# Interleaving the first two query passes of an attention kernel in halves of the keys, with the second half projected later

## The chip, the cores and the metric

One core of one Trainium2 chip. The kernel before takes 510.46 us (510.23 to 510.75). "Span" is what the profile shows of one execution on the core; it is shorter than the device time of the same execution by 1.7 us in nearly all of them (510.06 us and 508.4 us for the profiled execution of the kernel before).

Engines: TensorE (PE, with its weight loads PEld), VectorE (DVE), ScalarE (ACT), GpSimd (POOL), SyncE (SP, which issues the transfers).

## The reference

Two attention blocks over 2048 tokens, 448 wide, 16 heads of 28, put side by side. Cut to what matters here:

```python
def _A_ref(x, wqkv, wo):                       # part A: full softmax attention
    q, k, v = ...                              # x @ wqkv, split in 16 heads
    scores = einsum('bhqd,bhkd->bhqk', q, k) * Dh ** -0.5
    p = softmax(scores)
    return einsum('bhqk,bhkd->bhqd', p, v)... @ wo
# part B: 4 segments of 512 tokens, each with masked softmax attention inside
# the segment and a linear-attention memory of the segments before it
return concatenate([a, b], axis=-1)
```

## The kernel before

The kernel schedules itself. A model of the engines in Python runs while the program is built, and emits instructions in the order in which the model finds them ready; every engine then runs its list in order. The chip's times don't feed back.

Scores are handled in "banks" of 128 keys by 512 queries of one head, 1184 in all: 1024 for part A (16 passes, each 4 heads by 512 queries by 16 key tiles) and 160 for part B. Most banks go to ScalarE, which takes the exponential of three and two banks in turn (`NBS`). Some, called vbanks, go to VectorE, which computes the exponential from integer and polynomial steps over pairs of banks. Three slots of PSUM, the memory that holds TensorE's results, serve everything else: accumulators of a pass, projections, and vbanks.

```python
NBS = (3, 2)
YB = 3          # buffers of a pair of vbanks; shared with the tiles of x (xn)
AHEAD = 12      # a side piece may run this many banks ahead of its place
SEM = 45        # model: ns for a semaphore
SLACK = 300
HEADQ = 2
LASTV = 18      # no vbank from a pass with fewer free banks than this
...
    order = []                                  # order of the score banks
    for n, (kind, a, b) in enumerate(SEQ):      # SEQ: (A,0,0), (A,0,1), (A,0,2), ...
        T[kind, a, b] = len(order)
        if kind == "A":
            order += [("A", a, b, kt, j) for kt in range(NT) for j in range(4)]
        ...
    def fuse(bs):                               # may the last score group be joined by vbanks?
        used = {b[4] for b in bs}
        if sum(x["pos"] < 0 for x in side_work) > HEADQ:   # head pieces still open
            return
        for _ in range(2):
            if backlog(m["top"]) > BACKLOG: return         # VectorE has enough to do
            s = free_slot(m["top"])
            if s is None: return                           # no PSUM slot
            b = vbank_pick(used)                           # buffers; LASTV; 24 of a pass at most
            if b is None: return
            emit_vbank(b, s)
...
    # what the first pass needs: transposes of x (t_piece), keys, values, queries
    head = [kq_piece("k", "A", 0, 0, P, 2 * P), kq_piece("k", "A", 0, 0, 2 * P, CW),
            t_piece(1, 0), t_piece(1, 1), k_("A", 0, 1),
            v_piece("A", (0, 1), 0), v_piece("A", (2, 3), 0),
            t_piece(2, 0), t_piece(2, 1), k_("A", 0, 2),
            v_piece("A", (4, 5), 0), v_piece("A", (6, 7), 0),
            t_piece(3, 0), t_piece(3, 1), k_("A", 0, 3)]
    head += [v_piece("A", (t, t + 1), 0) for t in range(8, 16, 2)] + [q_("A", 0, 1)]
    spread(head, -100, -50)                     # places before the first bank: at once
```

After the last scores, `last_step` and `last_finish` accumulate the last pass (tile `acc`, copied to `osb`), normalise it and multiply by the output weights (`y_mm`).

The softmax here doesn't subtract the row's maximum and nothing guards it: scores larger than these inputs give would overflow.

## Time and profile before

| | kernel before |
|---|---|
| time, median | 510.46 us |
| span of the profiled execution | 508.4 us |
| ScalarE busy | 492.9 us (97%) |
| TensorE / VectorE busy | 475.4 (94%) / 445.7 us (88%) |
| first exp starts | 8.32 us |
| exps on ScalarE | 211 of three banks, 210 of two, 1 of one = 1054 banks |
| vbanks on VectorE | 130 |

First the windows view of the kernel before: a row for each stretch of time, with its length, then the busy time and (in brackets) the instructions of each engine, the granted clock of TensorE (the share of its full clock that the profile reports), the DMA share and GB/s.

```profile
8.00:40.00 32.00, 31.69 (x380) 14.78 (x377) 15.08 (x25) 31.25 (x28) 8.42 (x17) 1.00 0.28 68
40.00:300.00 260.00, 243.42 (x2573) 83.23 (x2572) 246.97 (x410) 260.00 (x234) 67.94 (x79) 1.00 0.13 32
300.00:490.00 190.00, 180.18 (x1783) 61.79 (x1786) 170.62 (x318) 189.00 (x172) 60.03 (x91) 1.00 0.20 56
```

The order of the engines is PE, PEld, DVE, ACT, POOL. ScalarE (fourth) is busy 260.00 of 260.00 us in the long middle. VectorE (third) is idle for half of the first stretch, in which TensorE is full.

Then ScalarE's groups of instructions by shape: count, busy time of the group, mean length of one, and the idle time before them.

```profile
L561 ACT ACTIVATE pt<-ps_s 128x1536 bf16<-128x1536 f32 x211 | 326.6, 1548 | 1.8 <-PE ps_s L280 1.3 <-PE ps_v_5806 L280 0.4
L561 ACT ACTIVATE pt<-ps_s 128x1024 bf16<-128x1024 f32 x210 | 237.1, 1129 | 0.1
...
L561 ACT ACTIVATE pt<-ps_s 128x512 bf16<-128x512 f32 x1 | 0.7, 672 | 0.0
```

The three groups sum to 564.4 us, while all exps together kept ScalarE busy for 480.4 us: in the trace one exp overlaps the next, by an estimated 0.2 us (84 us over 421 changes from one to the next). So the lengths can't simply be added.

And ScalarE's timeline, cut to the rows in which it was idle before an exp or before the last accumulation: start, length of the run of instructions, and in brackets the idle time before it with what ended it.

```profile
8.32 6.88 ACT L561 ACTIVATE pt<-ps_s 128x1536 bf16<-128x1536 f32 x6 [0.53 <-PE ps_s L280]
15.54 53.63 ACT L561 ACTIVATE pt<-ps_s 128x1536 bf16<-128x1536 f32 x47 [0.33 <-PE ps_s L280]
...
336.12 6.88 ACT L561 ACTIVATE pt<-ps_s 128x1536 bf16<-128x1536 f32 x6 [0.40 <-PE ps_v_5806 L280]
...
412.33 85.61 ACT L561 ACTIVATE pt<-ps_s 128x1536 bf16<-128x1536 f32 x76 [0.47 <-PE ps_s L280]
500.43 0.78 ACT L1195 COPY osb<-acc 128x128 f32<-128x128 f32 x4 [2.48 <-PE acc L280]
```

This gives an account of the whole span. It has four terms:

- **start**: until the first exp, 8.32 us;
- **stalls** of ScalarE between first and last exp: 0.33 + 0.40 + 0.47 = 1.20 us;
- **tail**: from the end of the last exp (500.43 - 2.48 = 497.95 us) to the end of the span, 10.45 us;
- **net work**: the rest, 488.43 us, in which ScalarE runs its exps and a few other activations without a pause that this view shows.

### The profile page before, as it was taken

The numbers are of one execution on the slowest core, as the hardware profiler recorded it, in microseconds if no ns is written. First come the engines' busy times: TensorE is split into PE (matmuls) and PEld (weight loads), VectorE is DVE, ScalarE is ACT, GpSimd is POOL, SyncE is SP. The second block draws the span as 40 slices with busy tenths as digits, with TensorE's granted clock in tenths as the row PEclk, the third lists the DMA queues.
The fourth block names the chain that finished last, engine by engine and source line by source line (L and its number), as shares of the span: only waits on it lengthen the run. The fifth ranks groups of instructions, "written<-read, shape, count | busy, mean of one in ns | idle before, by whom it ended". The sixth has DMA issues, their size and how long they took to land.

```text
span 508.4 us, 12361 instructions
## 1 busy us (share of the span) xinstructions
PE 475.4 (94%) x4918; PEld 168.6 (33%) x4918; DVE 445.7 (88%) x777; ACT 492.9 (97%) x450; POOL 144.6 (28%) x199
## 2 busy tenths in 40 slices
PE   8999999999999999999889999899999999999996
PEld 5443233343332333333223333433333333333332
DVE  4349999999999999989989989879979958998993
ACT  5999999999999999999999999999999999999993
POOL 8202211221122110351260431372161183202110
PEclk9999999999999999999999999999999999999999
DMA  9200000000033100022021102012312120312112
GB/s 249 56 1 5 22 13 13 3 22 4 23 109 73 37 9 3 23 66 48 20 66 46 44 6 65 23 31 65 101 52 57 50 76 18 108 50 60 39 48 65
DMA packets 42178, 23.76 MB, mean 47 GB/s; under 512 B 22636, under 2 KB 37804, under 8 KB 42120
## 3 DMA queue, kind: packets, MB, share of 16 engines
q1 hardware_dynamic: 40808, 21.72, 16.1%
q0 software_dynamic: 416, 0.81, 0.7%
q8 instruction: 38, 0.62, 0.5%
q10 hardware_dynamic: 896, 0.45, 0.3%
q14 instruction: 20, 0.16, 0.1%
HBM read 16.58 MB, written 4.28 MB: 41 GB/s over the span
## 4 chain that ended last, share of the span: by engine, by line
ACT 52%; PE 22%; issue 19%; DVE 5%; POOL 1%; DMA 1%; DVEq 0%; ACTq 0%; POOLq 0%
ACT pt L561 50%; PE ps_s L280 6%; PE acc L280 5%; PE ps_proj L280 3%; PE ps_v L280 2%; PE ps_y L280 2%; ACT phiq L1042 1%; PE ps_kn L280 1%; PE ps_warm L219 1%; DVE vy L458 1%; DVE y L1080 1%; POOL pt L579 1%; DVE vz L505 1%; DVE oT L753 1%; PE ps_t L1022 0%
## 5 line engine op out<-in xcount | busy, mean ns | idle before, releaser
L561 ACT ACTIVATE pt<-ps_s 128x1536 bf16<-128x1536 f32 (+1 forms) x422 | 480.4, 1337 | 2.0 <-PE ps_s L280 1.3
L280 PE MATMUL ps_s<-qTA,kTA 28*128 28x512 bf16 x894 | 141.1, 383 | 20.3 <-ACT pt L561 17.4
L513 POOL TENSOR_SCALAR vz<-vy 128x1024 f16<-128x1024 uint16 x59 | 71.0, 1203 | 290.6 <-DVE vy L458 147.0
L280 PE MATMUL acc<-pt,vA 128*32 128x512 bf16 x894 | 116.8, 386 | 0.0
L280 PEld LDWEIGHTS <-kTA 28*128 28x128 bf16 x1024 | 46.4, 91 | 144.1 <-issue 140.0
L495 DVE SCALAR_TENSOR_TENSOR ve<-vy,vz 128x1024 uint16<-128x1024 int32 x65 | 80.8, 1243 | 0.1
L579 POOL TENSOR_SCALAR_AFFINE_SELECT pt<-pt 128x256 bf16<-128x256 bf16 (+3 forms) x112 | 59.5, 559 | 54.4 <-ACT pt L561 54.3
L280 PE MATMUL acc<-warm 128*32 128x512 bf16 (+1 forms) x634 | 68.5, 384 | 0.0
L506 DVE TENSOR_TENSOR vz<-vz,vl 128x1024 f16<-128x1024 f16 x65 | 50.1, 770 | 0.1
L280 PEld LDWEIGHTS <-vA 128*32 128x32 bf16 x1024 | 31.7, 94 | 47.8 <-issue 41.1
L505 DVE TENSOR_TENSOR vz<-vz 128x1024 f16<-128x1024 f16 x65 | 47.2, 726 | 0.2
L280 PE MATMUL ps_proj<-xT_100,wst 128*32 128x512 bf16 x512 | 38.3, 383 | 0.1
L280 PE MATMUL ps_proj<-xT_99,wst 128*32 128x512 bf16 (+2 forms) x512 | 37.1, 374 | 0.3 <-DVE vy L458 0.2
L280 PE MATMUL acc<-ve,vA 128*32 128x512 bf16 x130 | 33.5, 383 | 0.0
L280 PEld LDWEIGHTS <-wst 128*32 128x32 bf16 x1024 | 22.4, 95 | 28.2 <-issue 18.4
L280 PE MATMUL ps_s<-qTB,kTB 28*128 28x384 bf16 (+3 forms) x256 | 25.7, 299 | 5.0 <-ACT pt L561 4.2
L509 DVE TENSOR_SCALAR vl<-vz 128x1024 f16<-128x1024 f16 x65 | 27.3, 420 | 1.2 <-POOL vz L513 1.2
L720 DVE COPY osb<-acc 128x512 f32<-128x512 f32 x31 | 21.2, 683 | 7.0 <-PE acc L280 7.0
L280 PEld LDWEIGHTS <-warm 128*32 128x32 bf16 (+1 forms) x642 | 18.9, 94 | 21.5 <-issue 15.3
L753 DVE TENSOR_TENSOR oT<-osb,bc 128x512 bf16<-128x512 f32 x31 | 24.7, 797 | 0.0
L280 PE MATMUL acc<-pt,vB 128*32 128x128 bf16 (+3 forms) x256 | 20.5, 303 | 0.6 <-POOL pt L579 0.4
L280 PE MATMUL ps_y<-woB,oT 128*128 128x448 bf16 x80 | 20.7, 356 | 0.2
(388 smaller groups left out, 496.9 us busy)
## 6 DMA issues: line engine op xcount, KB each, us to landing
out_dram<-y SPq DMA_DIRECT2D x31, 112.0 KB
xn<-in_A_x_dram SPq DMA_DIRECT2D x3, 448.0 KB
wst<-in_A_wqkv_dram SPq DMA_DIRECT2D x2, 249.0 KB
woA<-in_A_wo_dram POOLq DMA_DIRECT2D x4, 98.0 KB, 7.2
woB<-in_B_wo_dram POOLq DMA_DIRECT2D x4, 98.0 KB, 4.5
wst<-in_A_wqkv_dram SPq DMA_DIRECT2D x1, 336.0 KB
wst<-in_B_wv_dram SPq DMA_DIRECT2D x1, 336.0 KB
wst<-in_B_wk_dram SPq DMA_DIRECT2D x1, 336.0 KB
```

Of the source, the lines that this page charges most:

```text
L219: nc.tensor.matmul(wps[:], lhsT=warm[:, 0:P], rhs=warm[:], start=True, stop=True)
L280: nc.tensor.matmul(out, **kw)
L458: dve(e0, 0, 533, lambda: nc.vector.tensor_scalar(out=pr["y"][:, i, :], in0=ps[:], scalar1=Y1, scalar2=Y0, op0=ALU.mult, op1=ALU.add), aft ...
L495: step(t, 533 * n, lambda: nc.vector.scalar_tensor_tensor(out=ef.bitcast(U16), in0=y, scalar=2.0 ** -9, in1=z, op0=ALU.mult, op1=ALU.add), ...
L505: step(t, 267 * n, lambda: nc.vector.tensor_mul(z, z, z), lambda t: step(t, 267 * n, lambda: nc.vector.tensor_mul(z, z, l), whole))
L506: lambda t: step(t, 267 * n, lambda: nc.vector.tensor_mul(z, z, l), whole))
L509: step(t, 133 * n, lambda: nc.vector.tensor_scalar(out=l, in0=z, scalar1=Z3, scalar2=Z2, op0=ALU.mult, op1=ALU.add), square)
L513: eng.tensor_scalar(out=z, in0=y.bitcast(U16).rearrange("p (c t) -> p c t", t=2)[:, :, 0], scalar1=2.0 ** -16, scalar2=Z0, op0=ALU.mult, o ...
L561: nc.scalar.activation(out=pt[:, 0:n, :], in_=ps[:, 0:n, :], func=ACT.Exp, scale=scale)
L579: nc.gpsimd.affine_select(out=blk, in_=blk, compare_op=ALU.is_ge, fill=0.0, base=0, pattern=pat, channel_multiplier=-1)
L720: nc.vector.tensor_copy(out=os_[0][:], in_=a[:])
L753: nc.vector.tensor_mul(get_oT(side, s)[:, g, :], os_[0][:], bc[:])
```

## The change

The first two query passes of part A use the same keys and values. The change runs them interleaved: pass 0 with the first eight key tiles, pass 1 with the first eight, then pass 0 and pass 1 with the last eight. So keys and values of the second half are needed 32 banks later, and their transposes and projections leave the crowded head. TensorE gets room there, and VectorE may start on vbanks earlier. Since x tiles and vbank pairs share buffers, the count of used buffers (`ys`) starts at 3 and falls as each x tile has been transposed.

```diff
+SPLIT = 8
...
+    first = order[:128]
+    half = [[b for b in first if b[2] == cq and (b[3] < SPLIT) == lo] for cq in range(2)
+            for lo in (True, False)]
+    order[:128] = half[0] + half[2] + half[1] + half[3]
...
-    st = {"u": 0, "pos": 0, "ys": 0, "es": 0, "work": 0.0, "nrm": 0, "ot": 0}
+    st = {"u": 0, "pos": 0, "ys": 3, "es": 0, "work": 0.0, "nrm": 0, "ot": 0}
...
                 rt["x", "A", r, half] = e
+                st["ys"] -= half
...
-            t_piece(1, 0), t_piece(1, 1), k_("A", 0, 1),
-            v_piece("A", (0, 1), 0), v_piece("A", (2, 3), 0),
-            t_piece(2, 0), t_piece(2, 1), k_("A", 0, 2),
-            v_piece("A", (4, 5), 0), v_piece("A", (6, 7), 0),
-            t_piece(3, 0), t_piece(3, 1), k_("A", 0, 3)]
-    head += [v_piece("A", (t, t + 1), 0) for t in range(8, 16, 2)] + [q_("A", 0, 1)]
+            t_piece(1, 0), t_piece(1, 1), v_piece("A", (0, 1), 0), k_("A", 0, 1),
+            v_piece("A", (2, 3), 0), q_("A", 0, 1), v_piece("A", (4, 5), 0), v_piece("A", (6, 7), 0)]
     spread(head, -100, -50)
+    head = [t_piece(2, 0), t_piece(2, 1), k_("A", 0, 2), t_piece(3, 0), t_piece(3, 1)]
+    head += [v_piece("A", (8, 9), 0), k_("A", 0, 3)]
+    head += [v_piece("A", (t, t + 1), 0) for t in range(10, 16, 2)]
+    spread(head, 8, 8 * SPLIT + 8)
```

## The prediction

> **What bounds the kernel now.** ScalarE. The page gives it 492.9 us busy of a 508.4 us span (97%), almost all of it one group: 422 exp activations, 480.4 us. The windows view says where it is not busy: before its first exp at 8.32 us; 0.43 us between 8.32 and 40 us; nothing between 40 and 300; 1.0 us between 300 and 498; and 8.2 of the last 10.45 us, where it waits for the last accumulation (2.5 us in the waits view) and the closing matmuls. So the time is the start, plus ScalarE's exp work, plus its few stalls, plus the tail. VectorE (88%) takes 130 of the 1280 score banks off ScalarE. It is idle in one place only: between 8.32 and 40 us it is busy 15.1 of 31.7 us, waiting (waits view) 7.6 us for value projections and about 6 us for key/query projections. TensorE is then the busy one (31.4 of 31.7 us). From 40 us on VectorE is 93% busy.
>
> **What the change does.** With the first two query passes interleaved in halves of the keys, transposes and projections of the second key half are needed 32 banks later. Comparing the two built programs by matmul order: in the first 64 banks, 248 side matmuls in place of 284; the VectorE exps begin in the first 64 (5 banks; none before), stand at 14 against 11 after 128 and at 30 against 28 after 256. The catch: the lead does not last. After 640 banks both stand at 74, and the totals are 131 against 130. ScalarE keeps 211 three-bank and 210 two-bank exps and loses only the single one-bank exp. Projections, the passes' closing work, masks (110 instructions, the same number of blocks) and DMA are equal in number; 27 filler matmuls are added, in TensorE's slack. The gain goes back because the later picks are limited by buffers, by VectorE's backlog and by a cap per pass, not by how many banks were done early.
>
> **Cost.** By shapes, a three-bank exp takes 1548 ns, a two-bank one 1129 ns: 419 ns a bank. The Trainium skill, "ScalarE: Activation LUTs", section "What ACT_TABLE_LOAD costs", says 0.833 ns per element (427 ns for 512); the trace agrees. The 422 exps take 480.4 us for 1150 banks, which leaves an estimated 0.4 to 0.5 us for the lost bank with its instruction. All of that is on the critical path. The 0.43 us of early stalls, one of 0.33 us at 15.5 us, may go as well, as TensorE has less to do there. The first exp comes after the same instructions, so the start stays. VectorE's 17 us of early idle time are worth little: they are used now, but VectorE gets them back as slack later, off the path.
>
> The tail changes form: ScalarE's last unit has three banks in place of one, and VectorE's last piece is a half pair. I allow 1 us either way. The schedule behind the head is reshuffled too; new small stalls of ScalarE, as before 0 to 2 us, I put at 0.3 us.
>
> **Predicted:** 510.55 - 0.5 - 0.4 + 0.3, about 509.9 us; range 508.5 to 511.5. Faster by over 2%: 0.01; within 2%: 0.97; slower by over 2%: 0.02.
>
> **Right or wrong in the profile.** Right: first exp at 8.3 us; 421 exps, about 479.9 us; VectorE busy well over 15 us between 8 and 40 us, and less busy later; ScalarE gaps between first and last exp within 0.5 to 2 us; tail after the last exp 9.5 to 11.5 us. Wrong: a gap of over 1 us in ScalarE between 8 and 50 us, ended by score matmuls that stood behind a projection or a value tile waiting for VectorE or its PSUM slot, since two accumulators are held at once there and leave one slot of three.

Two figures in it are wrong and are put right here. "1280 score banks" and "1150 banks" counted score matmuls; a bank of part B can take two. There are 1184 banks, of which ScalarE has 1054 before. So the exps cost 480.4 / 1054 = 0.456 us a bank, and the "640" in the text is a count of matmuls too. The conclusions drawn from them about the lost bank don't change.

## More of the kernel before

The metric is the device time of one execution in microseconds, as the median of several executions.

Output projections of earlier passes (tile `ps_y`) are side pieces.

## The result

| | before | changed |
|---|---|---|
| time, median | 510.46 us (510.23 to 510.75) | 508.82 us (508.60 to 509.42) |
| ratio | | 0.9969 (0.9952 to 0.9987) |
| span of the profiled execution | 508.4 us | 506.9 us |
| ScalarE's banks | 1054 | 1053 |

A ratio is the mean time of one kernel's runs over that of the other's of the same rounds, so it isn't quite the ratio of the medians. The time fell by 1.6 us, 0.3%: inside the range of the prediction, and further than its centre of 509.9 us.

The windows of the changed kernel, with the same columns:

```profile
8.00:40.00 32.00, 30.74 (x363) 14.19 (x364) 23.66 (x39) 30.93 (x28) 10.55 (x19) 1.00 0.29 68
40.00:300.00 260.00, 245.03 (x2614) 84.23 (x2616) 245.72 (x406) 259.96 (x235) 67.30 (x80) 1.00 0.13 32
300.00:490.00 190.00, 180.70 (x1786) 61.72 (x1793) 171.13 (x318) 189.81 (x173) 59.61 (x89) 1.00 0.20 56
```

VectorE is busy 23.66 us in the first stretch, 8.6 us more. That is the intent fulfilled. ScalarE's busy time in that stretch did not change to match, because it was full before as well.

Its groups and idle rows:

```profile
L566 ACT ACTIVATE pt<-ps_s 128x1536 bf16<-128x1536 f32 x211 | 327.3, 1551 | 1.3 <-PE ps_s L281 1.1
L566 ACT ACTIVATE pt<-ps_s 128x1024 bf16<-128x1024 f32 x210 | 237.7, 1132 | 0.0
```

```profile
8.86 6.89 ACT L566 ACTIVATE pt<-ps_s 128x1536 bf16<-128x1536 f32 x6 [0.53 <-PE ps_s L281]
16.29 54.41 ACT L566 ACTIVATE pt<-ps_s 128x1536 bf16<-128x1536 f32 x48 [0.54 <-PE ps_s L281]
...
498.88 0.77 ACT L1201 COPY osb<-acc 128x128 f32<-128x128 f32 x4 [1.43 <-PE acc L281]
```

The account in the four terms (us, profiled executions):

| | start | net work | stalls | tail | span |
|---|---|---|---|---|---|
| before | 8.32 | 488.43 | 1.20 | 10.45 | 508.4 |
| changed | 8.86 | 488.05 | 0.54 | 9.45 | 506.9 |
| difference | +0.54 | -0.38 | -0.66 | -1.00 | -1.5 |

So with one bank fewer ScalarE's net work is 0.38 us less (the busy time of its exps fell from 480.4 to 479.9 us), and the two larger terms lie 300 us and more behind the place of the change: two stalls in part B (at 336 and 412 us) are gone, and the tail is shorter. The head's own stall did not go. It grew from 0.33 to 0.54 us.

**The start is not the change's doing.** TensorE's list is the same in both kernels up to the first scores. In the groups that read the x tiles (count, then least, median and greatest length in ns, and first and last start), the kernel before shows:

```profile
L227 PE MATMUL ps_h_171<-ident,xn x4: 219/267/314, 4.7 to 5.4; 128*128 128x128 bf16 x4
...
L227 PE MATMUL ps_h_174<-ident,xn x4: 219/219/219, 5.2 to 5.7; 128*128 128x128 bf16 x4
```

and the changed kernel:

```profile
L228 PE MATMUL ps_h_171<-ident,xn x4: 314/314/314, 4.7 to 5.6; 128*128 128x128 bf16 x4
...
L228 PE MATMUL ps_h_174<-ident,xn x4: 314/314/314, 5.3 to 6.3; 128*128 128x128 bf16 x4
```

The same transposes take 219 ns in one execution and 314 ns in another, from the start or from some transpose on. The Trainium skill, "TensorE: Matmul & The Clock Gate", section "What's actually happening", says that the clock of a cold TensorE doubles after a busy window that runs freely, so that the moment varies by about 500 ns either way between executions. The profiles agree: over the 14 kernels profiled the first exp starts between 7.97 and 8.92 us, with no clear order by kernel (8.32 to 8.92 us with the old head, 7.97 to 8.86 us with the new one). The start follows the mean length of the 16 transposes: 219 ns goes with 7.97 to 8.06 us (three profiles), 314 ns with 8.77 to 8.92 us (four, two of each kernel). The kernel before also spread over 507.9 to 509.1 us of span in its own runs. So a difference in one pair of profiles carries about half a microsecond of this either way.

### The profile page after: what moved, and what is told of

Read it like the earlier page. It is cut to its first block, busy times and chain, and to the rows that moved or that the text cites. A ratio compares the mean times of both kernels' runs of the same rounds, so it can differ in the third digit from the quotient of the medians.

```text
span 506.9 us, 12393 instructions
## 1 busy us (share of the span) xinstructions
PE 475.3 (94%) x4936; PEld 168.8 (33%) x4945; DVE 450.0 (89%) x782; ACT 492.5 (97%) x449; POOL 144.4 (28%) x200
## 4 chain that ended last, share of the span: by engine, by line
ACT 55%; issue 20%; PE 19%; DVE 4%; POOL 1%; DVEq 0%; ACTq 0%
ACT pt L566 54%; PE ps_s L281 5%; PE acc L281 4%; PE ps_proj L281 4%; PE ps_y L281 2%; PE ps_v L281 1%; ACT phiq L1048 1%; DVE vy L463 1%; PE ps_warm L220 1%; POOL pt L584 1%; DVE ve L500 0%; DVE vB L832 0%; DVE phik L877 0%; DVE vz L510 0%; DVE vz L511 0%
## 5 line engine op out<-in xcount | busy, mean ns | idle before, releaser
L566 ACT ACTIVATE pt<-ps_s 128x1536 bf16<-128x1536 f32 (+1 forms) x421 | 479.9, 1342 | 1.3 <-PE ps_s L281 1.1
L518 POOL TENSOR_SCALAR vz<-vy 128x1024 f16<-128x1024 uint16 (+1 forms) x60 | 74.5, 1242 | 295.3 <-DVE vy L463 166.0
L500 DVE SCALAR_TENSOR_TENSOR ve<-vy,vz 128x1024 uint16<-128x1024 int32 x66 | 84.3, 1280 | 0.2
L584 POOL TENSOR_SCALAR_AFFINE_SELECT pt<-pt 128x256 bf16<-128x256 bf16 (+3 forms) x112 | 55.7, 525 | 47.7 <-ACT pt L566 47.0
L281 PE MATMUL acc<-warm 128*32 128x512 bf16 x628 | 68.1, 384 | 0.3
L510 DVE TENSOR_TENSOR vz<-vz 128x1024 f16<-128x1024 f16 x66 | 48.5, 737 | 0.3
L281 PE MATMUL acc<-ve,vA 128*32 128x512 bf16 x131 | 35.9, 383 | 0.0
L281 PE MATMUL ps_s<-qTB,kTB 28*128 28x128 bf16 (+3 forms) x256 | 25.4, 299 | 5.5 <-ACT pt L566 4.8
L1086 DVE CAST y<-ps_y 128x448 bf16<-128x448 f32 x28 | 17.3, 619 | 6.2 <-PE ps_y L281 5.8
L758 DVE TENSOR_TENSOR oT<-osb,bc 128x512 bf16<-128x512 f32 x31 | 21.6, 697 | 0.0
L281 PE MATMUL acc<-pt,vB 128*32 128x384 bf16 (+3 forms) x256 | 21.2, 303 | 0.4 <-POOL pt L584 0.2
```

The source lines that it names most:

```text
L281: nc.tensor.matmul(out, **kw)
L500: step(t, 533 * n, lambda: nc.vector.scalar_tensor_tensor(out=ef.bitcast(U16), in0=y, scalar=2.0 ** -9, in1=z, op0=ALU.mult, op1=ALU.add), ...
L510: step(t, 267 * n, lambda: nc.vector.tensor_mul(z, z, z), lambda t: step(t, 267 * n, lambda: nc.vector.tensor_mul(z, z, l), whole))
L518: eng.tensor_scalar(out=z, in0=y.bitcast(U16).rearrange("p (c t) -> p c t", t=2)[:, :, 0], scalar1=2.0 ** -16, scalar2=Z0, op0=ALU.mult, o ...
L566: nc.scalar.activation(out=pt[:, 0:n, :], in_=ps[:, 0:n, :], func=ACT.Exp, scale=scale)
L584: nc.gpsimd.affine_select(out=blk, in_=blk, compare_op=ALU.is_ge, fill=0.0, base=0, pattern=pat, channel_multiplier=-1)
```

## The experiments

All of them change the order that the builder makes, so each was checked by its built program first (banks on each engine, last units), and these counts are in the expectations. Each was timed in five rounds beside the kernel before on the same chip. All twelve gave correct results.

### 1. Is it the early vbanks? VectorE kept out of the first 64 banks

```diff
         used = {b[4] for b in bs}
+        if st["pos"] < 64:
+            return
```

> The changed kernel, but VectorE may take no score bank while fewer than 64 banks have been passed. Built, VectorE takes 127 banks in all (changed kernel 131, before 130), so ScalarE has 4 more than in the changed kernel. Theory (the early banks are what the change earns): 4 banks at about 0.45 us each come back, 510.3 to 511.0 us, the VectorE idle time between 8 and 40 us returns in part. Rival (the gain is relief of TensorE in the head, or a luckier tail, and the early VectorE banks do not matter): within 0.5 us of the changed kernel, 508.5 to 509.3 us.

Measured: 512.41 us (512.31 to 516.71), the kernel before 510.40; ratio 1.0060 (1.0034 to 1.0086). VectorE's busy time in the first stretch fell to 12.94 us:

```profile
8.00:40.00 32.00, 31.75 (x362) 15.25 (x359) 12.94 (x21) 31.40 (x28) 7.38 (x16) 1.00 0.28 69
```

The rival is out: in this schedule, without the early vbanks, the kernel is slower than the kernel before by 2 us. The theory's sign was right and its size too small. Against the changed kernel, net work rose by 2.05 us for 4 banks, about as expected (1.8 us), and that alone is more than the gain of 1.64 us. The tail rose by 1.57 us and the stalls by 0.28 us, which had not been foreseen; the reshuffles below show that these two also move when nothing of substance is changed.

### 2. The interleaved order alone, with the old head

```diff
-            t_piece(1, 0), t_piece(1, 1), v_piece("A", (0, 1), 0), k_("A", 0, 1),
... (the head of the kernel before in place of that of the changed kernel)
+    head += [v_piece("A", (t, t + 1), 0) for t in range(8, 16, 2)] + [q_("A", 0, 1)]
```

> The interleaved order of the changed kernel with the old list of head pieces (all transposes, keys and values of the first pass at the old place). Built, VectorE takes 130 banks as before. Theory (interleaving alone earns nothing, only the deferral of head work that it permits): 510.2 to 511.5 us, with a ScalarE stall at the first bank of the second pass, as its query projection stands last in the list. Rival (the interleaving itself helps, by spreading the work): 508.5 to 509.5 us.

Measured: 517.99 us (517.78 to 518.22); ratio 1.0153 (1.0140 to 1.0166). ScalarE's waits (who ended them, total, times, longest):

```profile
ACT pt L566 <- PE ps_v L281: 8.6, 1, 8.6
```

TensorE's timeline before that wait ended:

```profile
24.14 1.71 PE L281 MATMUL ps_v<-wst,xT 128*128 128x224 bf16 x16
25.78 0.39 PE L281 MATMUL acc<-pt,vA 128*32 128x512 bf16 x2
25.80 1.23 PE L281 MATMUL ps_proj<-xT,wst 128*32 128x512 bf16 x16
26.97 1.80 PE L281 MATMUL ps_v<-wst,xT 128*128 128x224 bf16 x16
28.69 1.05 PE L281 MATMUL ps_proj<-xT,wst 128*32 128x512 bf16 x16
29.67 0.39 PE L281 MATMUL ps_s<-qTA,kTA 28*128 28x512 bf16 x2
```

The scores of the second pass stand behind the whole old head, because their query projection is its last piece. The Trainium skill, "PSUM — Partial Sum Buffer", section "Engine vs sequencer instructions", says that matmuls start and complete in program order; here that costs one stall of 8.57 us. The rest of the account (net 487.90, tail 11.27 us) adds up to about that of the kernel before: without this stall the span would be 507.8 us by subtraction, against 508.4. The direction was expected, the size was not (510.2 to 511.5 us): a stall had been foreseen, but not how long. So the interleaved order with this list loses by the place of one piece. A list with that query projection moved forward and nothing deferred was not run, so it isn't shown that interleaving alone earns nothing.

### 3. Two more vbanks for the changed kernel

```diff
-LASTV = 18
+LASTV = 17
```

> The changed kernel with the limit for picks in the last pass lowered from 18 free banks to 17. Built, VectorE takes 133 banks (131), ScalarE ends with a one-bank unit as the kernel before does. Theory (time is ScalarE's banks at 0.45 us plus the tail after its last exp): work 0.9 us less; the tail of 9.5 us may grow back to 10.5 us as before: 507.6 to 509.0 us. Rival (the count does not matter, the half pair in the tail does): slower than the changed kernel by about 1 us, 509.5 to 510 us.

Measured: 508.39 us (507.71 to 510.02); ratio 0.9971 (0.9956 to 0.9985), so it can't be told from the changed kernel. Net work fell by 1.25 us to 486.80, and the tail rose by 0.93 us to 10.38. Both parts of the theory came as said, and they nearly cancel.

### 4. The changed kernel's totals with the old head

```diff
-LASTV = 18
+LASTV = 16          # in the kernel before
```

> The kernel before with the limit for picks in the last pass lowered from 18 to 16. Built, it has the totals and the last units of the changed kernel (131 banks, last exps of 3, 2 and 3 banks), with the old head. Theory: what counts is the number of banks and the tail, wherever they are taken: about 508.8 to 509.7 us, close to the changed kernel. Rival (the head itself is faster in the changed kernel, whatever the count): 510.0 us or more.

Measured: 513.75 us (513.58 to 513.88); ratio 1.0069 (1.0057 to 1.0081). With the same 131 vbanks and the same last units as the changed kernel it is 5 us slower than that. Net work is 488.28 us, as the count says, but the theory's number (508.8 to 509.7 us) was far off, and the time lies where the rival put it (510.0 us or more). The account doesn't bear the rival out either: the start is within 0.06 us of the changed kernel's, the stalls are 1.90 us, 1.36 more (one of 1.04 us at 257 us), and the tail is 13.10 us, 3.65 more. So the tail is not given by the last units. ScalarE's waits:

```profile
ACT osb L1195 <- PE acc L280: 5.0, 1, 5.0
```

and TensorE's timeline from the last scores on:

```profile
497.01 0.39 PE L280 MATMUL ps_s<-qTA,kTA 28*128 28x512 bf16 x3
497.34 0.40 PE L280 MATMUL acc<-pt,vA 128*32 128x512 bf16 x4
497.67 1.69 PE L280 MATMUL ps_y<-woA,oT 128*128 128x448 bf16 x8
499.28 0.82 PE L280 MATMUL acc<-pt,vA 128*32 128x512 bf16 x10
499.74 0.38 PE L280 MATMUL acc<-ve,vA 128*32 128x512 bf16 x1
500.05 1.69 PE L280 MATMUL ps_y<-woA,oT 128*128 128x448 bf16 x8
502.45 1.30 PE L1130 MATMUL ps_y<-woA,oT 128*128 128x448 bf16 x6 [0.71 <-DVE y L1080]
503.67 0.39 PE L280 MATMUL acc<-ve,vA 128*32 128x512 bf16 x2
```

Behind the last scores stand 22 output-projection matmuls (`ps_y`) ahead of the last accumulation. In the changed kernel there are 7:

```profile
495.27 0.39 PE L281 MATMUL ps_s<-qTA,kTA 28*128 28x512 bf16 x3
495.60 0.40 PE L281 MATMUL acc<-pt,vA 128*32 128x512 bf16 x4
495.93 0.36 PE L281 MATMUL ps_y<-woA,oT 128*128 128x448 bf16 x1
496.22 0.40 PE L281 MATMUL acc<-pt,vA 128*32 128x512 bf16 x4
497.00 0.73 PE L1136 MATMUL ps_y_8554<-woA,oT 128*128 128x448 bf16 x3 [0.38 <-DVE y L1086]
497.57 0.73 PE L1136 MATMUL ps_y_8558<-woA,oT 128*128 128x448 bf16 x3
498.23 0.39 PE L281 MATMUL acc<-ve,vA 128*32 128x512 bf16 x1
498.23 0.60 PE L281 MATMUL acc<-pt,vA 128*32 128x512 bf16 x5
```

The same count in the kernel before is 11 (timeline cut to the scores, the `ps_y` and the end):

```profile
496.38 0.39 PE L280 MATMUL ps_s<-qTA,kTA 28*128 28x512 bf16 x1
496.69 1.12 PE L280 MATMUL ps_y<-woA,oT 128*128 128x448 bf16 x5
...
498.56 0.73 PE L1130 MATMUL ps_y_8522<-woA,oT 128*128 128x448 bf16 x3 [0.20 <-DVE y L1080]
499.13 0.73 PE L1130 MATMUL ps_y_8526<-woA,oT 128*128 128x448 bf16 x3
499.79 0.40 PE L280 MATMUL acc<-pt,vA 128*32 128x512 bf16 x3
500.01 0.38 PE L280 MATMUL acc<-ve,vA 128*32 128x512 bf16 x1
```

Six of each count (L1130 or L1136) are the last pass's own, which `last_step` puts there in all 14 versions; what differs are the leftovers of earlier pieces: 16 here, 5 in the kernel before, 1 in the changed kernel. This became the new theory of the tail: it is TensorE's leftover queue, above all output projections that were not done before the last scores, together with what they wait for on VectorE.

### 5 and 6. The last pass alone

The limit for picks changed in the last pass only leaves everything before it as it was. The changed kernel without its lone 131st vbank:

```diff
-            if i == n and len(free) < LASTV:
+            if i == n and len(free) < (LASTV if i < len(SEQ) - 1 else 20):
```

> The changed kernel, with the limit for VectorE picks raised from 18 to 20 free banks in the last pass alone. The built program is that of the changed kernel up to the last 23 of ScalarE's banks; then VectorE does not take the lone 131st bank, so both engines have the totals of the kernel before (130 banks, 1054 on ScalarE, last exp of one bank). It undoes what the change did to the tail and to the total, and leaves its head. Theory (start, work, stalls and tail add up, and the head earns no time of itself): work plus 0.4 us; tail after the last exp 9.5 to 10.5 us; 508.9 to 510.2 us. Rival (the early banks in the head save time directly): stays within 0.2 us of the changed kernel.

Measured: 508.18 us (507.44 to 508.53), the kernel before 509.92; ratio 0.9959 (0.9946 to 0.9971). ScalarE is given one bank back, as many as in the kernel before, and the time doesn't rise. Net work 488.89 (+0.84 against the changed kernel), tail 8.73 us (-0.72), stalls 0.81 (+0.27), start 7.97 (-0.89); 6 output matmuls are left. The theory's range is missed on the low side: the tail shrank beyond the 9.5 us that it gave as the least. The rival (within 0.2 us of the changed kernel) is missed on the same side, by 0.64 us. The account says why the time didn't rise: the tail gave back nearly all that the bank cost. Rebuilding both programs confirms that they are alike but for the last 2% of TensorE's instructions. So the start and the new stall (at 443 us) are scatter between two executions, and probably also what net work rose beyond one bank (0.46 us): some 0.3 to 0.4 us in a term.

The kernel before with a lone 131st vbank:

```diff
-            if i == n and len(free) < LASTV:
+            if i == n and len(free) < (LASTV if i < len(SEQ) - 1 else 8):
```

> The kernel before with the limit for picks in the last pass alone lowered from 18 to 8 free banks: a lone 131st bank is taken there, so it has the totals and the last units of the changed kernel, and the old head. Theory: work minus 0.4 us, but the lone bank is taken late and its chain on VectorE lies after the last exps, as the lowered limit in all passes showed (5.0 us from last exp to accumulation): tail 12 us or more, total 511 us or more. Rival (totals and last units decide): about 509 us.

Measured: 511.32 us (510.90 to 511.52); ratio 1.0020 (1.0006 to 1.0034). Net work 488.17 (-0.26), stalls as before (1.21), tail 11.53 us (+1.08), with 14 output matmuls left in place of 11. The time is as expected; the tail is a little shorter than the 12 us given. The expected mechanism is in the trace: TensorE has done its output matmuls and runs fillers (`warm`), and the last accumulation waits for the lone vbank's values (`ve`) from VectorE:

```profile
500.10 0.60 PE L280 MATMUL acc<-warm 128*32 128x512 bf16 x4
501.15 0.38 PE L280 MATMUL acc<-ve,vA 128*32 128x512 bf16 x1 [0.45 <-DVE ve L495]
```

So a lone bank taken from ScalarE late is no gain in either kernel: it saves 0.3 to 0.8 us of work and costs 0.7 to 1.1 us of tail.

### 7 to 10. Is the gain a property of the change? The same pair, reshuffled

Small changes of the model's constants leave the work alone and reshuffle the order of everything. Two such changes were made to both kernels.

```diff
-SEM = 45
+SEM = 46
```

> The kernel before with one constant of its schedule changed from 45 to 46, which reshuffles the order neutrally. Built, VectorE takes 129 banks (130). If the difference of the two kernels is a systematic gain of 2 to 3 banks and the kernel before is a lucky member of its family: 510.5 to 512.5 us. If reshuffling hardly matters: within 0.5 us of the kernel before.

> The changed kernel with the same neutral reshuffle (45 to 46). Built, VectorE takes 132 banks (131). Systematic gain: 507.5 to 509.5 us, and 1.5 to 3 us below the reshuffled kernel before. If the gain was a matter of luck in the tail: the pair differs by less than 0.5 us, or the other way round.

```diff
-AHEAD = 12
+AHEAD = 13
```

> A second neutral reshuffle of the kernel before: pieces of projection work may be taken 13 banks ahead of their place, not 12. Built, VectorE takes 128 banks (130), ScalarE 1056. From the bank count alone, at 0.45 us a bank: 0.9 us above the kernel before, 511.3 us. From what the first pair of reshuffles showed (stalls of 0.4 to 2.5 us and tails of 8.7 to 11 us after the last exp outweigh the count): anywhere between 509.5 and 513 us.

> The changed kernel with the same reshuffle (13 banks ahead). Built, VectorE takes 131 banks, ScalarE 1053, 3 fewer than the reshuffled kernel before. Theory now (the change earns a bank count of 1 to 3 on ScalarE, 0.5 to 1.4 us, and the rest of the difference of any pair is stalls and tail, which come out either way): the pair differs by minus 3 to plus 2 us, while the net exp work differs by minus 1.0 to minus 1.8 us. Rival (the change shortens the stalls or the tail as a rule): minus 1.5 us or more.

Measured (medians of five; the pairs of a row share a chip and its runs of the kernel before, 509.92 us in the second row and 510.21 us in the third):

| | before | changed | difference | ScalarE's banks | output matmuls left |
|---|---|---|---|---|---|
| as given | 510.46 | 508.82 | -1.64 | 1054, 1053 | 11, 7 |
| SEM 46 | 510.11 | 511.94 | +1.83 | 1055, 1052 | 14, 11 |
| AHEAD 13 | 513.65 | 509.62 | -4.03 | 1056, 1053 | 15, 10 |

The expectation for the first reshuffled pair, a gain of 1.5 to 3 us, failed: its sign is the other way, as the alternative (luck in the tail) allowed, although by the account it was stalls and not the tail that turned it. The kernel before with SEM 46 stayed within 0.5 us of the kernel before; with AHEAD 13 it came out above its whole range (509.5 to 513 us). The expectation for the second pair (-3 to +2 us) failed on the other side, where the rival stood (-1.5 us or more); its part on net work (-1.0 to -1.8 us) held. In neither can the time of the pair be had from the bank count. The accounts (us):

| | net work | stalls | tail |
|---|---|---|---|
| before, SEM 46 | 489.42 | 0.39 | 11.01 |
| changed, SEM 46 | 488.00 | 2.54 | 10.71 |
| before, AHEAD 13 | 490.10 | 1.54 | 11.67 |
| changed, AHEAD 13 | 488.54 | 1.12 | 10.27 |

The profiled execution of the first row was the slowest of its five (511.45 us, with a granted clock of 0.948), so its terms aren't those of the median; but the stalls are clear. ScalarE's waits of the changed kernel with SEM 46, 2.5 us in four waits, the one before the first exp (0.53 us) included:

```profile
ACT pt L566 <- PE ps_s L281: 2.5, 4, 1.1
```

against 0.9 us in two, counted the same way, in the kernel before with SEM 46:

```profile
ACT pt L561 <- PE ps_s L280: 0.9, 2, 0.5
```

What holds in all three pairs, with that reservation about the second: the changed kernel leaves ScalarE 1 to 3 banks fewer, its net work is lower (-0.38, -1.42, -1.56 us), and its tail is shorter, with 3 to 5 output matmuls fewer left over. What does not hold is the stalls: -0.66, +2.15, -0.42 us.

### 11 and 12. Looking for a version that beats both

```diff
-LASTV = 18
+LASTV = 17
-            if i == n and len(free) < LASTV:
+            if i == n and len(free) < (LASTV if i < len(SEQ) - 1 else 20):
```

> The version with the limit of 17 in all passes (133 VectorE banks, 508.4 us), with the limit raised to 20 in the last pass alone, so that the lone 133rd bank is left to ScalarE: 132 banks. Theory (a lone late bank costs the tail more than its 0.45 us; dropping it from the changed kernel shortened the tail from 9.45 to 8.73 us): tail from 10.4 to about 9.3 us, net work plus 0.5 us, 507.0 to 508.4 us. If the tail does not follow: 508.5 to 509 us.

Measured: 508.61 us (508.36 to 509.38), the kernel before 510.21; ratio 0.9968 (0.9955 to 0.9980). The tail did not follow: 11.01 us, with 10 output matmuls left where experiment 3 left 9. Leaving the lone bank to ScalarE doesn't shorten the tail as such; in experiment 5 the list behind the last scores had become shorter with it, by one output matmul, eight accumulations and a wait of 0.38 us for VectorE, and here it had not.

```diff
-SLACK = 300
+SLACK = 310
-            if i == n and len(free) < LASTV:
+            if i == n and len(free) < (LASTV if i < len(SEQ) - 1 else 22):
```

> A third reshuffle of the changed kernel (the slack that a ready time must have, 310 ns in place of 300), with the lone last bank left to ScalarE: 132 banks, the last exp of two banks. By count and tail alone 507.5 to 508.5 us; with the new stalls of an untried order, up to 512 us.

Measured: 508.98 us (508.81 to 509.16); ratio 0.9973 (0.9960 to 0.9985), stalls 0.54, tail 10.38 us with 11 output matmuls left. That is above the range by count and tail alone, although no new stall came.

Five versions of the changed kernel thus lie between 508.2 and 509.0 us, and their intervals overlap; its two plain reshuffles, 509.62 and 511.94 us, lie above. The lowest, experiment 5, has the ratio 0.9959 against 0.9969 of the changed kernel; the intervals don't separate them. No version clearly beats the changed kernel.

### What the accounts have in common

Over all 14 profiles a straight line through net work against ScalarE's banks has a slope of 0.55 us a bank (correlation 0.94). A line through the wait from the last exp to the last accumulation against the output matmuls left behind the last scores has a slope of 0.23 us each (correlation 0.92), from 6 matmuls with 0.61 us to 22 with 5.01 us. This is a correlation, and no run removes output matmuls alone. In experiments 5 and 6 only the last pass differs, and the wait moves in the same direction as the count (7 to 6: 1.43 to 0.61 us; 11 to 14: 2.48 to 3.50 us), but other things moved with it: in 5, eight accumulations and a wait of 0.38 us; in 6, the chain of the lone vbank on VectorE.

The length of the last exp counts as well. In the kernel before the last exp (one bank) ends 1.18 us after the last scores, and in the changed kernel (three banks) 1.79 us; the last accumulation is done 3.66 and 3.22 us after them. So of the 1.05 us by which the wait shortened, 0.61 us is the longer last exp, behind which more of TensorE's list is hidden, and 0.44 us the shorter list. After the wait the tail is the same in all 14 profiles, 7.97 to 8.12 us.

## Why the prediction was right or wrong

- **The time: right, in part by luck.** 508.82 us lies in the range, and the change is far inside 2%. But of the terms only the lost bank came as said; both stall terms had the wrong sign, and the tail made most of the gain. With SEM 46 the same change gave 511.94 us, outside the range.
- **"ScalarE is the bound", and early VectorE time is worth little in itself: right.** VectorE gained 8.6 us of busy time in the first stretch, and ScalarE's total fell by one bank.
- **The lost bank, 0.5 us: right** (421 exps with 479.9 us of busy time, as named; 0.38 us of net work). But one bank is a net of two things. Without the early vbanks the count is 127 (experiment 1), so in these schedules the early vbanks carry 4 and the rest of the change costs 3 again. In the builder, the refusals of a vbank after the first 64 banks for want of a PSUM slot rose from 176 to 213, and those for VectorE's backlog fell from 131 to 105. So the limit that grew is the PSUM slot, which the prediction named at most as one of its "buffers"; the backlog that it named eased, and the cap per pass hardly occurs. This is a count of the builder, confirmed by rebuilding both programs, and not a run.
- **The early stalls, 0.4 us, "may go": wrong.** The stall at 15.5 us grew to 0.54 us, and all eight versions profiled with the new head had it with 0.54 us, against 0.33 to 0.39 us in the six with the old one.
- **"New small stalls, 0 to 2 us, I put at 0.3 us": wrong sign here.** The stalls behind the head fell from 0.87 us to none. The reshuffles show that such stalls are a draw: 0 to 2.0 us behind the head in the changed kernel's versions. The range was right, and the central value can't be had from the two programs.
- **The tail, "1 us either way", centre 0: the term that was mis-sized.** It fell by 1.00 us, the largest term of the gain. It came out just under the 9.5 to 11.5 us that the prediction named. Its reason, the shape of the last unit, holds for 0.61 us (the three-bank exp hides more of TensorE's list); the other 0.44 us is the list itself, with 7 output projections in place of 11, which could have been counted in the built programs before the run. The shape alone doesn't set the tail: the kernel before with the same last units waited 5.01 us in experiment 4 and 3.50 us in experiment 6.
- **"The start stays": right of the change**, but a profile's start varies by up to 0.95 us from execution to execution, which a comparison of two profiles must take off.

What is shown: the four terms in the profiles; that the gain was lost without the early vbanks, in the one schedule tried; that the interleaved order with the old head as it stood loses by one stall; that the tail can be moved by the last pass alone. What is argued from the lists and a correlation: that the leftover list sets the tail. What is open: why the changed order leaves fewer output projections for the end in all three pairs. Three pairs are too few to call it a rule, and no run separates it from chance.

## What to carry to other kernels

On a kernel that is already tuned to one saturated engine, account for the span as start, net work, stalls and tail of that engine before explaining a change of a fraction of a per cent; idle time filled elsewhere shows up only as work taken off that engine. Count in the built program what stands behind the last piece of the saturated engine's work, and see what that list waits for: in these runs the tail grew with it. And where a builder decides the order, test the change under a few neutral reshuffles, since a single pair can be +1.8 us or -4.0 us for the same idea.

## What the Trainium skill lacked or had wrong

- "TensorE: Matmul & The Clock Gate", section "Part 4: PE-mode transpose", says that the full clock does not engage for transposes. The 16 transposes at the start of this kernel took 314 ns each in one execution, and 219 ns each, all 16, in another (experiment 5); in the kernel before they went from 314 to 219 ns within the row. So, whatever their clock, they don't keep one length. Eight warm-up matmuls stand before them, so these runs don't test whether transposes by themselves count as work that raises the clock.
- The same page gives the variation of the warm-up as about 500 ns either way. The first exp behind it started between 7.97 and 8.92 us over 14 profiles, in agreement; the page doesn't speak of the granted clock that this profile reports, which reads 1.00 in these stretches all the same (1.00 from 4 to 8 us in the kernel before and in the changed kernel), so that only the lengths of the matmuls show it.
- "ScalarE: Activation LUTs", section "What ACT_TABLE_LOAD costs": 0.833 ns per element makes 427 ns for 512 elements, and the trace shows 419 ns, 2% less, so nothing is wrong there. In the stream of alternating sizes a bank cost 0.456 us by the groups and 0.55 us by the slope over 14 profiles; whether the skill's figures give that was not worked out here.
